# Feed-forward and transposes as pairs of 64-row tiles, read-out levels as 64x64 tiles, early inverses by doubling, with a new instruction order

## The chip, the core and the metric

The kernel runs on one core of a Trainium2 chip. A core has five engines with instruction streams of their own: TensorE (PE) for matrix products, whose weight loads the profile lists apart as PEld; VectorE (DVE); ScalarE (ACT); GpSimd (POOL); and SyncE (SP), which here only issues DMAs. They synchronise through semaphores. PE writes its results to PSUM, and DVE and ACT bring them from there to SBUF. The metric is device time in microseconds (us), the median of several runs.

## The reference

The first half is a recurrence over 768 tokens, for 4 batches of 8 heads (32 sequences), with a 40x40 state for each:

```python
for t in range(S):
    y[:, :, t] = np.einsum('bhd,bhde->bhe', rt, state)
    Sa = np.einsum('bhde,bhe->bhd', state, at)
    state_decay = state * wt[:, :, None, :] - np.einsum('bhd,bhe->bhde', Sa, bt)
    state = state_decay + np.einsum('bhd,bhe->bhde', vt, kt)
```

The second half takes `y` as 3072 rows of 320 numbers and is a gated feed-forward with 1536 hidden units:

```python
rms = np.sqrt(np.mean(x * x, axis=-1, keepdims=True) + 1e-06)
xn = x / rms * rms_g
g = xn @ w_gate
silu = g * (1.0 / (1.0 + np.exp(-g)))
val = xn @ w_val
return (silu * val @ w_out).astype(np.float32)
```

The four weight inputs are 64-bit floats and everything else is 32-bit. The kernel turns the weights into 32-bit floats itself.

## The kernel before

**Chunks.** The tokens are cut into 24 chunks of C = 32. For each chunk, all 32 sequences are handled together: a tile's 128 partitions hold two halves (`half`, 64 partitions) of two sets of 32 tokens, or 40-wide vectors at partitions 0 to 39 and 64 to 103 (`part`).

`front(c)` prepares a chunk. It loads w, a, k, b, v by DMA, transposes them on PE (`turned`, eight transposes of 128 rows in one piece called a turn), and makes Gram products (`gramk`, 32 products of 40 rows by 64 columns in each of four pieces), from which DVE picks, with `where`, the 32x32 triangular matrix `LT` of each sequence, level by level (`LEVELS` = 1, 2, 4, 8, 16). Between levels DVE and ACT scale and copy the decayed keys `K` and `A`.

`inverse(c)` inverts the triangular matrices by forward substitution on DVE, 31 steps of two operations each, with DMAs through DRAM that put one sequence on each row and back. For the first four chunks (`EARLY`) `early_inverse(c)` does two halves of 16 so, 15 steps, and joins them on PE with two pieces of small products.

`main(c)` applies a chunk. On PE it makes the pieces "state", "lower" (twice), "update", three turns (r, every second chunk; `VU`; the state `ST`), "score", five read-out "level" pieces and "y0". A level piece multiplies 128 rows: `As` holds the masked scores of both halves with zeros between (`msi` is the mask), so 16 products of 128 rows and 40 columns do a level. `down` adds the levels into `y` on DVE. Then `y` is transposed (`turn4`), normalised on ACT, and transposed again (`turn3`) into `xg`.

**Feed-forward.** `feed(g)` takes the 256 rows of two chunks. There are 12 slices of 128 hidden units, two at a time. For each slice the weights (480 KB) come by DMA from `sW` in DRAM. The 320 inputs are two full blocks of 128 rows and one of 64: the pieces "h64" (gate and value side by side as two 64-row tiles) and "h" (four products of 128 rows), with 256 columns moving. ACT makes the Silu, DVE multiplies (`hT`), and "out" adds two products of 320 moving columns into the PSUM tile `po`. A product of 32-bit floats shows in the trace as two matmul records, a transpose as one.

**Narrowing.** `narrow` makes the 32-bit weights, in 24 pieces of 480 columns: DMA in, three ACT operations, three DVE operations, and DMA out to `sW`. `narrow_slice(f)` is called from the first `feed`.

**What sets the order.** Nothing is issued where it is written. `Plan.add` records each piece with what it reads and writes, and `Plan.issue` plays all pieces in the order of a table of numbers, `ORDER`; a "-" there is a warm-up product on PE (line 1015). `PAIRS` says which of three double PSUM banks (`ps`) a piece uses. Engines take their instructions in that order, each waiting on semaphores. Since helper functions issue everything, the profile names few lines: 444 for DVE's tensor operations, 467 and 470 for ACT's copies and scalings, 486 for products, 489 for transposes, 483 for DMAs.

Of the kernel before, what the change touches and what calls it, by code (L numbers as in the profile page):

```python
# [21 lines left out]
WB = 5  # L22
LEAD = 2
# [10 lines left out]
85 83 84 76 58 78 86 74 73 59 60 75 5 89 61 88 77 4 43 6 201 7 87 334 90 44 8 214 213 53 62 9 - - - - - - - - 93 18 10  # L34
567 335 557 11 12 13 79 14 15 94 566 80 210 16 95 558 108 17 200 - - - 97 96 19 20 100 21 2 22 101 23 98 25 568 202 24
26 107 112 57 - - - - - 102 106 111 124 27 209 122 392 103 109 52 119 113 104 54 578 569 577 155 199 125 110 105 204
120 - - - - - - 114 203 118 117 121 559 211 598 589 562 46 131 129 132 45 560 212 597 563 588 561 123 115 136 586 384
133 134 - - - - - 126 130 116 47 564 3 145 216 394 383 135 336 128 137 48 144 143 141 91 587 219 142 51 570 127 1005
565 146 138 337 55 573 579 281 393 220 582 608 571 390 234 239 607 572 583 580 380 574 251 222 38 221 609 575 581 42 -
- - - - - - - 223 82 226 339 64 379 227 338 39 81 139 224 263 149 576 238 153 56 249 247 590 206 584 228 382 237 591  # L40
593 272 40 233 232 381 154 0 593 32 139 390 204 228 591 388 234 249 247 - - 324 235 35 31 27 244 229 146 147 259 281
245 258 149 34 325 594 36 33 270 155 243 62 605 584 598 230 - 239 40 214 599 601 242 628 64 49 91 627 602 30 626 1135
600 28 48 257 603 29 241 68 150 255 65 0 1347 194 0 194 84 173 0 - - - 182 540 200 0 184 1 186 542 540 0 506 0 457 469
849 199 455 242 111 97 110 112 96 51 61 439 460 458 122 50 243 0 0 255 242 0 709 104 470 242 120 246 259 708 57 247
458 456 0 257 718 256 470 242 0 716 265 487 486 0 268 0 0 265 101 473 0 262 277 0 273 0 236 0 260 0 269 0 242 461 - -
- - - - - 237 0 240 0 278 242 252 0 242 252 0 90 0 0 98 99 246 0 0 230 440 0 230 94 93 457 440 231 - - - - - - - - -
240 441 244 0 44 0 468 440 255 0 450 468 269 469 0 257 214 439 238 213 203 0 257 203 93 449 92 0 0 234 - - - - - - - -
245 437 0 250 262 0 464 246 247 436 260 245 446 258 259 469 244 - - 255 471 465 468 470 466 0 269 215 255 478 466 93
94 264 95 96 266 97 0 97 470 1 2 98 99 0 0 96 467 97 469 98 468 251 265 99 470 100 471 101 441 102 103 258 104 105 260
106 - - - - - - - - - - - 0 106 107 471 108 0 108 502 503 472 0 108 109 110 111 0 0 0 0 0 - - 13 0 16 562 572 146 571  # L50
561 147 14 142 143 374 15 13 355 - - - 25 386 358 0 358 386 388 16 25 387 389 390 70 79 17 391 28 191 147 355 356 80
148 149 359 0 68 28 2 29 149 0 149 34 150 29 151 187 24 25 31 152 33 153 188 391 393 32 154 35 390 392 358 0 0 152 40
187 153 27 154 155 156 33 157 158 159 160 161 34 162 36 163 164 37 165 41 391 38 42 392 39 394 561 166 395 393 552 0
42 559 549 548 395 209 0 549 560 42 165 210 43 44 211 427 428 395 - - - 565 166 45 167 557 168 0 565 566 168 739 0 522
# [189 lines left out]
class Plan:  # L244
# [17 lines left out]
    def foot(self, ap):  # L262
# [9 lines left out]
        if key not in self.masks:  # L272
# [4 lines left out]
            self.masks[key] = m  # L277
        return p, p + dims[0][1], self.masks[key]

    def add(self, engine, kind, issue, outs, ins):  # L280
        me = len(self.pieces)
        k = self.count.get(self.stage, 0)
        self.count[self.stage] = k + 1
# [85 lines left out]
def kernel(  # L369
# [440 lines left out]
    def main(c):  # L810
# [120 lines left out]
        if c % CG == 0:  # L931
            xg[c // CG] = xg_.next()
# [115 lines left out]
```

## Time and profile before

| | |
|---|---|
| median of 3 runs | 1065.89 us (1064.65 to 1071.17) |
| span of the profiled execution | 1060.6 us |
| first feed-forward's result leaves PSUM | 238.7 us |
| tenth, eleventh, twelfth | 953.6, 1014.0, 1055.2 us |
| TensorE clock granted, mean | 0.979 |

A row of a group has the line, engine, operation, the tile written and the tiles read, the shape (rows by columns of the weights, then partitions by elements of what moves) and the count; behind the bar stand the busy time in us, the mean duration of one in ns, and the idle time of the engine just before, with what ended it. A row of the timeline has the start in us, the length, and how many equal records were merged; in brackets is the idle time before and what ended it. "issue" there means that the engine waited for nothing that the profile shows. In a row by windows the engines stand in the order PE, PEld, DVE, ACT, POOL, then the granted clock, the busy share of the DMA engines and GB/s.

### The profile page before, as it was taken

The page shows a single profiled execution, that of the slowest core. Times are in us where ns is not written, and L with a number is a line of the kernel's source. Part 1 is how long each engine was busy: PE and PEld are TensorE (multiplying, and loading weights), DVE is VectorE, ACT ScalarE, POOL GpSimd, SP SyncE. Part 2 cuts the span into 40 slices and gives each one's busy share as a digit, 9 for nine tenths or more (in the row PEclk, how much of TensorE's full clock was granted, in tenths as well). Part 3 has the DMA queues.
Part 4 walks back from the last instruction along what each step waited for, and adds up shares of the span by engine and source line. Part 5 has one row for each costly group of instructions (what it writes and reads, how often), then busy time and mean ns, then how long its engine had stood idle before and what let it go on. Part 6 is the DMA issues. An engine that isn't in the chain of part 4 may idle for free.

```text
span 1060.6 us, 53494 instructions
## 1 busy us (share of the span) xinstructions
PE 1009.5 (95%) x23406; PEld 829.3 (78%) x23406; DVE 842.3 (79%) x2861; ACT 468.1 (44%) x1043; POOL 309.5 (29%) x554
## 2 busy tenths in 40 slices
PE   7868999999999999999999999999999999999997
PEld 6767777777888778787778778787777888787875
DVE  8978878776868988898898798989889899787411
ACT  6856666643543534434443444434344443431211
POOL 8824413120532241241233241340331331110000
PEclk9777998999999999999999999999999999999999
DMA  9965458766565483655565555574555555443252
GB/s 168 216 155 133 77 127 207 211 123 178 127 140 126 106 173 96 150 134 125 123 155 129 135 132 114 122 160 119 137 126 126 138 137 138 100 132 102 80 162 68
DMA packets 172457, 143.35 MB, mean 135 GB/s; under 512 B 125504, under 2 KB 143872, under 8 KB 172224
## 3 DMA queue, kind: packets, MB, share of 16 engines
q1 hardware_dynamic: 153856, 116.96, 42.9%
q0 software_dynamic: 16192, 22.64, 12.1%
q8 instruction: 184, 3.01, 1.2%
q10 hardware_dynamic: 2176, 0.33, 0.3%
q14 instruction: 49, 0.40, 0.1%
HBM read 123.86 MB, written 15.99 MB: 132 GB/s over the span
## 4 chain that ended last, share of the span: by engine, by line
PE 72%; DVE 8%; DMA 4%; ACT 3%; issue 3%; POOL 2%; SPq 1%; DVEq 0%; ACTq 0%; POOLq 0%
PE ps L486 50%; PE po L486 13%; PE ps L489 8%; DMA wf<-sW 2%; DVE LT L444 1%; DVE y L444 1%; DVE tmp L444 1%; POOL kbn L483 1%; DVE Yi L444 1%; DVE K L444 1%; SPq L483 1%; DMA sY<-Yi 1%; ACT VU L467 1%; PE po L1015 0%; DVE Ab L444 0%
## 5 line engine op out<-in xcount | busy, mean ns | idle before, releaser
L486 PE MATMUL ps<-xg,wf 128*128 128x256 f32 (+1 forms) x1728 | 353.5, 390 | 4.0 <-DVE xg L444 2.0
L486 PEld LDWEIGHTS ps<-xg,wf 128*128 128x128 f32 (+1 forms) x1728 | 261.4, 188 | 57.2 <-issue 15.0
L486 PE MATMUL po<-wf,hT 128*128 128x320 f32 x576 | 183.1, 449 | 0.1
L464 ACT ACTIVATE sg<-ps 128x256 f32<-128x256 f32 x144 | 53.6, 382 | 228.2 <-PE ps L486 224.9
L444 DVE TENSOR_TENSOR tmp<-Yi,M 128x60 f32<-128x60 f32 (+24 forms) x620 | 130.7, 211 | 19.1 <-DMA M<-sB 5.9
L444 DVE TENSOR_TENSOR Yi<-Yi,tmp 128x60 f32<-128x60 f32 (+24 forms) x620 | 129.7, 209 | 12.7
L483 POOL DMA_DIRECT2D VU<-in_v_dram x92 | 53.2, 584 | 274.1 <-PE ps L486 141.8
L486 PEld LDWEIGHTS po<-wf,hT 128*128 128x128 f32 x576 | 102.5, 191 | 35.7 <-issue 4.1
L444 DVE TENSOR_TENSOR hT<-ps,sg 128x256 f32<-128x256 f32 x144 | 59.7, 420 | 67.2 <-ACT sg L464 66.4
L444 DVE TENSOR_TENSOR K<-K,T 128x512 f32<-128x512 f32 (+1 forms) x192 | 93.4, 496 | 8.3 <-PE ps L486 5.8
L486 PEld LDWEIGHTS ps<-Ab,K 40*64 40x64 f32 x4608 | 77.2, 138 | 28.1 <-issue 10.5
L467 ACT COPY K<-K 128x256 f32<-128x256 f32 (+1 forms) x168 | 71.7, 443 | 58.4 <-PE ps L486 39.2
L486 PE MATMUL ps<-Ab,K 40*64 40x56 f32 x4608 | 87.2, 224 | 9.7 <-issue 3.8
L444 DVE TENSOR_TENSOR As<-ps,msi 128x256 f32<-128x256 f32 (+1 forms) x186 | 78.9, 476 | 14.4 <-PE ps L486 13.8
L467 ACT COPY KN<-ps 128x640 f32<-128x640 f32 x96 | 66.1, 690 | 53.5 <-PE ps L489 23.3
L483 POOL DMA_DIRECT2D kbn<-in_b_dram x92 | 53.3, 583 | 96.7 <-PE ps L486 94.3
L486 PEld LDWEIGHTS ps<-As,KN 128*40 128x40 f32 x3072 | 66.5, 124 | 15.7 <-issue 10.4
L483 POOL DMA_DIRECT2D kbn<-in_k_dram x92 | 53.6, 585 | 82.7 <-PE ps L486 82.6
L486 PE MATMUL ps<-As,KN 128*40 128x32 f32 x3072 | 73.2, 205 | 3.1 <-issue 2.5
L483 POOL DMA_DIRECT2D wn<-in_w_dram x92 | 51.6, 567 | 62.7 <-DVE tmp L444 24.1
L444 DVE TENSOR_TENSOR y<-y,ps 128x256 f32<-128x256 f32 x119 | 50.0, 420 | 16.2 <-PE ps L486 13.7
L444 DVE COPY_PREDICATED LT<-near,ps 128x384 f32<-128x384 uint32 (+2 forms) x72 | 52.2, 725 | 2.6 <-PE ps L486 2.0
(133 smaller groups left out, 1546.0 us busy)
## 6 DMA issues: line engine op xcount, KB each, us to landing
wf<-sW SPq DMA_DIRECT2D x144, 480.0 KB, 3.9
M<-sB SPq DMA_DIRECT2D x80, 128.0 KB, 4.1
rn<-in_r_dram SPq DMA_DIRECT2D x24, 160.0 KB, 5.4
sW<-ex SPq DMA_DIRECT2D x16, 240.0 KB, 3.4
out_dram<-o SPq DMA_DIRECT2D x48, 80.0 KB, 4.2
kbn<-in_k_dram POOLq DMA_DIRECT2D x92, 40.0 KB, 3.9
kbn<-in_b_dram POOLq DMA_DIRECT2D x92, 40.0 KB, 4.1
wan<-in_a_dram POOLq DMA_DIRECT2D x46, 80.0 KB, 4.9
```

Source lines behind the costliest of these rows:

```text
L444: plan.add("DVE", kind, lambda at: fn(at(o), *m(at)), [o], aps(*args))
L464: plan.add("ACT", "act", lambda at: nc.scalar.activation(at(o), at(a), f, **kw), [o] + aps(acc), [a])
L467: plan.add("ACT", "copy", lambda at: nc.scalar.copy(at(o), at(a)), [o], [a])
L483: plan.add(by, "dma", lambda at: queue.dma_start(out=o, in_=i), [o], [i])
L486: return o, lhsT, rhs, lambda at: nc.tensor.matmul(at(o), lhsT, rhs, start=start, stop=stop, skip_group_check=True)
L489: return o, i, ident, lambda at: nc.tensor.transpose(at(o), i, ident)
```

## The change

**Feed-forward.** The 320 inputs become five blocks of 64 (`KC`), and gate and value stand in the two halves of the partitions, so that each product has 64 rows and goes in a pair with the one of the other half. The value half meets its blocks in another order, so `xg` holds each block in both halves; three DMAs per two chunks copy them across. "out" becomes "oa" and "ob": each half of `hT`'s rows is multiplied apart, once for its own bank of `po` and once crossed.

```diff
-            pe("h64", [mm(h[e][:, q], wk[e][4][half(q)], x[half(q), 2, :], e == 0, False) for e in range(2) for q in range(2)],
-               [hh])
...
-                pe("h", [mm(h[e][:, q], wk[e][2 * q + kt], x[:, kt, :], False, kt == 1)
-                                           for q in range(2) for kt in range(2)])
-                act(sgs[:, e], h[e][:, 0], AF.Silu)
-                tt(hTs[:, e], h[e][:, 1], sgs[:, e], MUL)
-                pe("out", [mm(po[:, q, 0:DM], hTs[:, e, q * P:(q + 1) * P], wfs[e][:, 2 * P:2 * P + DM], f + e == 0, f + e == FT - 1)
-                                            for q in range(CG)])
+        def proj(k, cross, first, last):
+            wfs, hT = done[k]
+            return pe("o" + "ab"[cross], [mm(po[:, r ^ cross, 0:DM], hT[half(r), e * GT + (r ^ cross) * P:e * GT + (r ^ cross) * P + P],
+                                             wfs[e][half(r), KC * P:], first and e == 0, last and e == 1)
+                                          for e in range(2) for r in range(2)])
...
+                pe("h", [mm(hh[:, r, e * GT:(e + 1) * GT], wfs[e][half(r), s * P:(s + 1) * P], x[half(r), s], e == 0 and s == 0, e == 1 and s == KC - 1)
+                         for s in range(KC) for r in range(2)], [] if e else [hh], [Y[k - 2]] if e and k > 0 else [])
+            act(sg, hh[:, 0], AF.Silu)
+            tt(hT, hh[:, 1], sg, MUL)
+            Y[k - 1] = proj(k, k % 2, k == 0, False)
+            if k:
+                Y[k - 1] = proj(k - 1, k % 2, False, False)
+        copy(still, po[0:1, :, 0:1])
+        proj(KF - 1, 1 - (KF - 1) % 2, False, True)
```

```diff
+        if c % CG == CG - 1:
+            x = xg[c // CG]
+            dma(x[half(0), 1:4:2], x[half(1), 0:3:2])
+            dma(x[half(1), 1:4:2], x[half(0), 0:3:2])
+            dma(x[half(1), 4], x[half(0), 4])
```

**Transposes.** Each one is cut into its two halves of rows, 64 (or 40) each; `turn4` and `turn3` likewise.

```diff
-        pe("turn", [flip(ps[0:outs, at(n), 0:ins], t[0:ins, n, 0:outs], ident[0:ins, 0:ins]) for n in range(N)])
+        pe("turn", [flip(ps[0:outs, u, at(n), 0:w], t[by(u), n, 0:outs], ident[by(u), by(u)]) for n in range(N) for u in range(2)])
```

**Read-out levels and Gram products.** A level takes 32 products of 64 rows, 40 columns and 16 moving columns in place of 16 of 128 rows and 32 moving columns; `As` is half as large, its mask `ms` has no zeros, and `down` adds the three middle levels in two halves. The Gram products from level 4 on load 60, 56 and 48 columns in place of 64.

```diff
-            pe("level", [mm(ps[part(o), slot(n)], z["KN"][LEVELS[j]][:, kn_at(LEVELS[j], n, o)],
-                              As[:, j, o * N + slot(n)].rearrange("p i t -> p (i t)")) for n in range(N) for o in range(2)])
+            pe("level", [mm(ps[part(o), i, slot(n)], z["KN"][LEVELS[j]][half(i), kn_at(LEVELS[j], n, o)],
+                            As[half(i), j, o * N + slot(n)]) for n, i, o in each])
...
-            pe("gramk", [mm(gr[half(i), o, n, 0:16 + D], K[part(o), 2 * n + i].rearrange("p x s -> p (x s)"),
+            pe("gramk", [mm(gr[i * 64:i * 64 + 64 - l, o, n, 0:16 + D], K[part(o), 2 * n + i].rearrange("p x s -> p (x s)")[:, 0:64 - l],
```

**Early inverses.** The first four chunks' inverses are made by doubling, five rounds of two PE pieces and two DVE operations, with no DMA.

```diff
+        for j in range(len(LEVELS)):
+            ps = plan.room()
+            pe("inv", [mm(ps[other(i, n), o, n % 4 * C:(n % 4 + 1) * C], LT[other(i, n), o * N + slot(n)], YZ[other(i, n), o, 1, n % 4] if j else one(other(i, n)))
+                       for n, i, o in by_q])
+            tt(W, ps[:, :, 0:4 * C].rearrange("p o (m t) -> p o m t", m=4), msk[:, j:j + 1, None].to_broadcast((P, 2, 4, C)), MUL)
...
+            pe("inv", [mm(ps[other(i, n), o, at(w, n)], *[x[other(i, n), o, n % 4] if x is W or j else one(other(i, n)) for x in ((W, YZ[:, :, 0]) if w == 0 else (YZ[:, :, 0], W))])
+                       for w in range(ws) for n, i, o in by_q])
...
+            tt(yz, yz if j else eye32[:, None, None].to_broadcast((P, 2, 8, C)), ps[:, :, 0:ws * 4 * C].rearrange("p o (m t) -> p o m t", t=C), SUB)
```

**Narrowing and buffers.** A slice is narrowed in three pieces of 384, 256 and 320 columns in place of two of 480, `WB` (weight buffers) goes from 5 to 6, and Silu and product take both slices at once.

**Order.** `ORDER` and `PAIRS` are new throughout:

```diff
 ORDER = """
-85 83 84 76 58 78 86 74 73 59 60 75 5 89 61 88 77 4 43 6 201 7 87 334 90 44 8 214 213 53 62 9 - - - - - - - - 93 18 10
...
+492 8 9 10 11 - - - 12 - 13 14 15 16 17 18 19 20 21 649 401 - - - 22 - 48 - 36 487 499 - 500 46 498 - 58 - 59
...
```

On PE, in the middle of the program, around the turn of `VU` of one chunk, the order before reads (a row is a line, an operation, the tiles, the shape written, and how often it stands there in a row):

```order
692 L486 MATMUL po<-wf_167,hT_174 128x320 x2
693 L489 MATMUL ps_76<-ident,VU_114 104x128 x8
694 L486 MATMUL ps_75<-Ab_145,K_141 64x56 x32
695 L486 MATMUL ps_77<-VU_114,KN_0_133 40x40 x32
696 L486 MATMUL po<-wf_168,hT_175 128x320 x2
697 L486 MATMUL po<-wf_169,hT_175 128x320 x2
698 L489 MATMUL ps_76<-ident,ST_117 104x104 x8
699 L489 MATMUL ps_77<-ident,K_141 128x104 x8
700 L486 MATMUL ps_75<-Ab_144,K_142 64x56 x32
701 L486 MATMUL ps_77<-rE_154,vut_103 64x32 x32
702 L486 MATMUL ps_76<-xg_166,wf_170 128x256 x2
703 L486 MATMUL ps_76<-xg_166,wf_171 128x256 x2
```

The order now, at the turn of `VU` of such a chunk:

```order
758 L519 MATMUL po<-wf_174,hT_177 128x320 x2
759 L522 MATMUL ps_76<-ident,VU_115 104x64 x16
760 L519 MATMUL ps_77<-VU_115,KN_0_134 40x40 x32
761 L519 MATMUL ps_75<-Ab_146,K_142 56x56 x32
762 L519 MATMUL ps_76<-rE_155,vut_103 64x32 x32
763 L519 MATMUL ps_77<-Ab_145,K_143 48x56 x32
764 L519 MATMUL ps_75<-ST_118,aP_148 32x40 x32
765 L519 MATMUL ps_75<-VU_116,LT_120 32x40 x32
766 L519 MATMUL ps_76<-As_159,KN_0_131 40x16 x32
767 L519 MATMUL ps_76<-rE_155,Sd_137 40x32
```

Before, feed-forward pieces (`po`, `xg`) stand between the pieces of the chunk at rows 696, 697, 702 and 703; now none stands from row 759 on until row 786 (row 767 is the first of the 32 products of "y0", rows 784 and 785 are a level and a turn).

Near the start, on PE, an early inverse before is two pieces among warm-ups (`po<-ident`):

```order
37 L1015 MATMUL po<-ident 128x128 x11
38 L486 MATMUL ps_77<-M_148,LT_118 16x16 x32
39 L486 MATMUL ps_76<-M_148 32x16 x32
40 L1015 MATMUL po<-ident 128x128 x2
41 L486 MATMUL ps_75<-Xs_156,M_148 32x40 x32
```

Now it is a row of pieces of 32 and 64 products, with Gram pieces of other chunks between:

```order
23 L519 MATMUL ps_75<-ident,M_149 32x32 x32
24 L519 MATMUL ps_75<-M_149,ident 32x32 x32
25 L519 MATMUL ps_77<-VU_115,LT_119 32x40 x32
26 L519 MATMUL ps_75<-M_149,LT_119 32x32 x32
27 L519 MATMUL ps_77<-Ab_146,K_142 60x56 x32
28 L519 MATMUL ps_76<-M_149 32x32 x64
```

The number of small products ahead of a given place of the program rises by these.

On SP the copies of the swapped halves stand among the weight loads of the next feed-forward:

```order
150 L516 DMA M_150<-sB_182 32x1024 x3
151 L516 DMA xg_168<-xg_168 64x256
152 L516 DMA xg_168<-xg_168 64x2x256 x2
153 L516 DMA wf_172<-sW_66 128x960
154 L516 DMA wf_171<-sW_65 128x960
```

Before, no such rows exist; the loads of `M` and `wf` follow each other there.

More of the change, by code (lines that the diff above doesn't have):

```diff
@@ L494, in issue @@
                 s[3](at)
-        plan.add("PE", kind, issue, [s[0] for s in steps] + more, [x for s in steps for x in s[1:3]])
+        return plan.add("PE", kind, issue, [s[0] for s in steps] + more, [x for s in steps for x in s[1:3]], after)
     ident = const.tile([P, P], FP32, name="ident")
@@ L939, in feed @@
+    Y = {}
     def feed(g):
```

359 lines of the change are left out of this document (166 added, 193 removed), and 336 rows, old and new, of the table ORDER.

## The prediction

> **What bounds the kernel now.** The page comes first: its span, the share of each engine, the instruction queue, and the chain that ended last by engine.
>
> ```profile
> span 1060.6 us, 53494 instructions
> PE 1009.5 (95%) x23406; PEld 829.3 (78%) x23406; DVE 842.3 (79%) x2861; ACT 468.1 (44%) x1043; POOL 309.5 (29%) x554
> q8 instruction: 184, 3.01, 1.2%
> PE 72%; DVE 8%; DMA 4%; ACT 3%; issue 3%; POOL 2%; SPq 1%; DVEq 0%; ACTq 0%; POOLq 0%
> ```
>
> TensorE (PE) is busy for 95% of the span and 72% of the chain. A view by windows then cuts the span into a start, a middle and an end (for each engine its busy time and, as x, its records).
>
> ```profile
> 0.00:240.00 240.00, 210.30 (x5275) 180.01 (x5276) 194.83 (x616) 151.65 (x321) 101.34 (x198) 0.91 0.69 158
> 240.00:960.00 720.00, 704.10 (x16848) 575.11 (x16847) 612.86 (x2149) 298.75 (x682) 207.09 (x354) 1.00 0.55 132
> 960.00:1061.00 101.00, 95.13 (x1286) 74.20 (x1284) 34.58 (x96) 17.68 (x42) 1.10 (x2) 1.00 0.35 104
> ```
>
> In the middle PE is busy 704 of 720 us and VectorE (DVE) 613; a chunk has 256+64+160+64+64+64+128+51 = 851 PE records and a feed-forward 192, so two chunks with their feed-forward take 720x1,894/16,848 = 81 us. So PE sets the time, and what a PE record costs decides the change. That is read from the timeline, not from the mean of a group, since records overlap: I divide the distance between starts by the count. First the pure feed-forward at the end (weight loads, one per product).
>
> ```profile
> 1030.57 0.73 PEld L486 LDWEIGHTS ps<-xg,wf 64*128 64x128 f32 x8 [0.44 <-issue]
> 1031.64 0.83 PEld L486 LDWEIGHTS po<-wf,hT 128*128 128x128 f32 x4 [0.33 <-issue]
> 1032.55 5.21 PEld L486 LDWEIGHTS ps<-xg,wf 128*128 128x128 f32 x24
> 1037.79 2.02 PEld L486 LDWEIGHTS po<-wf,hT 128*128 128x128 f32 x8
> 1040.25 1.13 PE L486 MATMUL ps<-xg,wf 64*128 64x256 f32 x8
> ```
>
> Whole-array products go at (1037.79-1032.55)/24 = 0.218 us. The eight 64-row products take 1031.64-1030.57 = 1.07 us: four pairs at 0.218 are 0.87, so the two row halves do run together, and 0.20 is left for the change of tile shape ("issue" in the row).
>
> Then the small products, in the middle and near the start.
>
> ```profile
> 446.09 0.81 PE L486 MATMUL ps<-Ab,K 40*64 40x56 f32 x40
> 447.43 0.57 PE L486 MATMUL ps<-Ab,K 40*64 40x56 f32 x24 [0.53 <-issue]
> 447.82 0.81 PE L486 MATMUL ps<-VU,KN 64*40 64x40 f32 x64
> 448.56 1.99 PE L486 MATMUL ps<-xg,wf 128*128 128x256 f32 x8
> 450.39 1.04 PE L489 MATMUL ps<-ident,VU 128*104 128x128 f32 x8
> 451.36 0.57 PE L486 MATMUL ps<-Ab,K 40*64 40x56 f32 x24
> 452.54 0.81 PE L486 MATMUL ps<-Ab,K 40*64 40x56 f32 x40 [0.61 <-issue]
> 453.17 1.09 PE L486 MATMUL ps<-rE,vut 40*64 40x32 f32 x64
> ```
>
> ```profile
> 111.80 0.64 PE L486 MATMUL ps<-As,KN 128*40 128x32 f32 x22
> 112.85 0.99 PE L486 MATMUL ps<-As,KN 128*40 128x32 f32 x41 [0.41 <-issue]
> 113.65 0.20 PE L486 MATMUL ps<-As,kbn 128*40 128x32 f32 x1
> 113.67 0.20 PE L486 MATMUL ps<-As,KN 128*40 128x32 f32 x1
> 113.69 0.80 PE L486 MATMUL ps<-As,kbn 128*40 128x32 f32 x31
> 114.42 0.55 PE L489 MATMUL ps<-ident,x 128*128 128x128 f32 x3
> 114.89 1.18 PE L486 MATMUL ps<-As,KN 128*40 128x32 f32 x51
> 116.30 0.45 PE L486 MATMUL ps<-As,KN 128*40 128x32 f32 x13 [0.22 <-issue]
> ```
>
> Here is the row that decides. PE stops inside a run of equal products that wait for nothing ("issue"). From one stop to the next, 112.85 to 116.30, stand 41+1+1+31+3+51 = 128 records; from 447.43 to 452.54 stand 24+64+8+8+24 = 128 again. The instruction queue moved 184 transfers for 23,406 products, one per 127 products with their weight loads. So PE's instructions arrive in blocks of about 127 products, and where a block is used up before the next is there, PE stands. In the lower stretch nothing but supply ended the stops, and a block took 116.30-112.85 = 3.45 us, or 0.027 us a product. By themselves small products go faster: 64 in 448.56-447.82 = 0.74 us, 40 in 453.17-452.54 = 0.63, thus 0.012 to 0.016, and 0.014 is my mean. This kernel escapes since one product in ten belongs to the feed-forward at 0.2 us or more, and in its order these pieces stand among the small ones.
>
> **The change part by part.** First PE, as if instructions cost nothing.
>
> *Turns* (transposes). A chunk has 5x8+4+4+3 = 51 of them, 8 in 451.36-450.39 = 0.97 us with a change of shape, so 0.11 each, 24x51x0.11 = 135 us. They become 102 half as long, in pairs. A pair costs 0.055 if only the moving length counts, 0.11 if the load of 104 to 128 columns does. The run of 40 above loads, in each row half, 128 columns (two tiles of 64) per four products, in 4x0.016 = 0.063. I take 0.06: 24x51x(0.11-0.06) = 61 us less (bounds 0 and 67).
>
> *Changes of tile shape.* The order of all PE rows has 531 before and 443 now: 88x0.20 = 18 us less. The new order still alternates between 64x128 and 64x64, so no more goes.
>
> *Trimmed Gram products.* 64 load columns become 60, 56 and 48; at 0.063 us per 128 columns that is 16x56x0.063/128 = 0.44 us a chunk, 10 us.
>
> *Read-out levels.* 160 records a chunk become 320. Today 31 start in 114.42-113.69 = 0.73, thus 0.023 each, 3.7 us; the nearest row of the new shape is the 64x40 one, 0.74/64 = 0.0116, again 3.7 us. I take 0.
> The Trainium skill, page "TensorEngine Tiling (Array Packing)", section "Theoretical Speedup", promises up to 2x from a second small dimension; by it the levels would give 24x3.7/2 = 44 us, and the time would be 1078. The 64x40 row speaks against it: at 0.0116 a product four tiles take as long as two do now.
>
> *Feed-forward products.* Ten 64-row pairs replace eight whole products and two pairs; by the 1.07 us row a pair costs what a whole one does, so 0. Three copies per two chunks (the swapped halves) go on SP's queue; the next feed-forward waits for them, and in the order pieces of the previous feed-forward and of chunks still stand ahead of it. Cost 0; about 4 us each time if that cover were gone, as for a copy of this size on that queue:
>
> ```profile
> M<-sB SPq DMA_DIRECT2D x80, 128.0 KB, 4.1
> ```
>
> The copy into `still` puts one wait on ACT and then PE at each feed-forward's end; behind it are ACT's next copies and PE's last eight products of that feed-forward, and chunk pieces stand around both. Cost 0.
>
> *DVE.* The rows:
>
> ```profile
> L444 DVE TENSOR_TENSOR As<-ps,msi 128x256 f32<-128x256 f32 x144 | 54.1, 416 | 4.8 <-PE ps L486 4.2 <-ACT As L470 0.4
> L444 DVE TENSOR_TENSOR As<-ps,msi 128x512 f32<-128x512 f32 x42 | 28.4, 683 | 9.6 <-PE ps L486 9.6
> L444 DVE TENSOR_TENSOR hT<-ps,sg 128x256 f32<-128x256 f32 x144 | 59.7, 420 | 67.2 <-ACT sg L464 66.4
> L444 DVE TENSOR_TENSOR Ab<-Ab,T 128x128 f32<-128x128 f32 x96 | 27.0, 289 | 1.2 <-PE ps L486 0.3 <-ACT Ab L467 0.2
> ```
>
> As falls from 54.1+28.4 to 24x4x0.416+18x0.42 = 47.5 (-35); hT to 72x0.683 = 49.2 (-10.5); the level sums split at three levels, 72x(2x0.289-0.42) = +11. Narrowing the same elements in 36 instead of 24 pieces adds 12x3 steps, at most 12x3x0.289 = 10 us, in the start. DVE goes to about 808 to 818 us. Per two chunks of the middle it is 81x612.86/720 = 69 now, 66 then, below PE's 81-89/12 = 74. It doesn't take over.
>
> *Early inverses.* Their 30 short DVE steps and the DMA round trips become PE products, (5x32+4x64+32)x4 = 1,792 or 3,584 records instead of 512, all before the middle; their price is in the start, below.
>
> Sum without a limit on instructions: 61+18+10 = 89 us less. The start (5,275 records, about five chunks) keeps its waits, so 19/24 of it counts, 71.
>
> Now the supply. A chunk goes from 851 records to 256+64+320+64+64+64+128+102 = 1,062, a feed-forward from 192 to 336. All: 24x1,062+12x336+3,584+252 warm-ups, less what chunk 0 lacks, about 33,200, which is 261 blocks. Spread evenly they would fit: 261x3.45 = 900 us. The order doesn't spread them. In the old order only one stretch without a feed-forward piece is over 264 records, the one before the first feed-forward. In the new one 35 more are over 254, with 13,388 records together, and the one shown with the change, from row 759, is 608 long. A stretch starts with about one block in hand; beyond it a product costs 0.027 instead of 0.014: (13,388-35x127)x0.013 = 116 us more. Who waits for that: the ACT and DVE steps that empty PSUM, which have room (44% and 79% busy).
>
> The start, with the first feed-forward product and the warm-ups that fill its waits:
>
> ```profile
> 130.27 1.14 PE L486 MATMUL ps<-xg,wf 64*128 64x256 f32 x8
> L1015 PE MATMUL po<-ident 128*128 128x128 f32 x302 | 48.0, 311 | 3.7 <-DVE po L517 3.3 <-issue 0.4
> ```
>
> The old order has 2,828 records ahead of that product, at 130 us. The new one has 5,800: 5,800/127x3.45 = 158 us if supply ends last throughout, so +28; 0 if the waits that hold PE today stay the longer. I take +22.
>
> Sum: 1060.6-71+116+22 = 1128; the median of the runs shown (1065.89) lies 5.3 above the profiled span, so 1133. Some stops will fall where PE waits today (16 us of the middle), 11 of them say: 1122.
>
> **The rivals.**
>
> *Supply hides.* The stops inside runs are rare today (all "issue" before weight loads, changes of shape included):
>
> ```profile
> PEld ps L486 <- issue: 62.4, 157, 2.0
> ```
>
> If the blocks come in time whenever PE isn't starved for other reasons, the time is 1060.6-89+5 = 977 to 1060.6-71+5 = 995, with DVE at 66 of 74 us close behind, so 970 to 1000. It decides from the point at which 127 products take as long as their supply: above 0.027 a product nothing stops. Against it: stops exactly 128 records apart, and 35 stretches that run at half of that.
> The Trainium skill, "Runtime: NRT & Kernel Launch", section "Instruction fetch mechanics", says that instructions come in blocks of 256 into a buffer of two, and that the crossing is mostly hidden. The trace agrees with the blocks (184 transfers for 46,812 loads and products are 254 each) and, by the rows above, not with the hiding in runs of small products. Chance 0.17.
>
> *Supply and today's waits overlap more than I count.* Half of the 116 and nothing at the start: 1060.6-71+58 = 1048, 1053 as a median, 1025 to 1075. Chance 0.15, half of it within 1%.
>
> *Nothing overlaps.* Every small product is paid at 0.027: 29,200 records outside the feed-forward x0.027 = 788, and of feed-forward 144 slices x (10x0.218+4x0.27) = 470, with 0.27 from the eight of row 1037.79 less a change of shape: 1,258 us. It decides where feed-forward pieces are held by PSUM or by the swapped copies. Against it: a block is always fetched during a feed-forward piece. Chance 0.05; or the turns' pairs not halving, 1122+61 = 1183, chance 0.05.
>
> **How the numbers follow.** Forecast 0.58 (1080 to 1170: supply cost from 75 to 150, turns and levels by their bounds). Slower by over 1%, which is about what a measurement tells from no change: 0.58+0.10 = 0.68. Within 1%: 0.08. Faster: 0.17+0.07 = 0.24. The likeliest alone spans 1080 to 1170; for 8 in 10 the range reaches down into the second rival and up to the turns' bound, 1010 to 1185, and leaves out the hidden supply and the case where nothing overlaps, 0.2 at most.
>
> **What would show it.** About 261 instruction transfers; PE "issue" stops near 128 records apart inside runs of levels and Gram products, longest in the stretch after a feed-forward, near 150 us together against 62; turns of 16 in about 0.5 us; no shape stops inside a feed-forward. DVE busy near 808 us and no longer close to PE's bound. It is wrong if runs of several hundred small products pass at 0.014 us each, if the middle falls below 75 us per two chunks, or if DVE or a DMA ends the chain's waits.

## The result, and the profile after

The changed kernel takes 1385.51 us (median of 4, 1381.15 to 1395.61) against 1068.53 for the one before on the same chip: ratio 1.2975, 95% interval 1.2905 to 1.3046. The profiled execution spans 1379.6 us, 319.0 more than before. Forecast were 1122 us: slower was right, and so were the number and the spacing of the instruction blocks, but the size was too small by more than 250 us, beyond even the rival in which nothing overlaps (1258).

The page of the kernel after, the lines that answer to those of before:

```profile
span 1379.6 us, 72886 instructions
PE 1119.2 (81%) x33212; PEld 941.1 (68%) x33212; DVE 813.4 (59%) x2745; ACT 451.3 (33%) x1025; POOL 302.9 (22%) x532
q8 instruction: 260, 4.26, 1.3%
PE 64%; issue 17%; DVE 12%; DMA 3%; ACT 2%; POOL 1%; SPq 1%; DVEq 0%; ACTq 0%; POOLq 0%
```

The 260 instruction transfers and DVE's 813 us are as forecast. But "issue" is 17% of the chain where it was 3%, and PE is busy for 110 us more than before although it should have had less to do. To see why, I cut both spans at the first output product of the first feed-forward (139 us before, 214 after). These are the windows of the kernel before, then of the kernel after (us, then busy time and records of PE, PEld, DVE, ACT, POOL, then the granted clock, DMA share and GB/s):

```profile
0.00:139.00 139.00, 114.16 (x3108) 101.97 (x3108) 116.63 (x355) 91.68 (x192) 76.28 (x155) 0.86 0.68 144
139.00:1061.00 922.00, 895.37 (x20305) 727.35 (x20298) 725.63 (x2508) 376.40 (x852) 233.24 (x399) 1.00 0.55 134
```

```profile
0.00:214.00 214.00, 157.04 (x5972) 142.17 (x5974) 113.75 (x291) 95.87 (x212) 64.70 (x126) 0.66 0.44 98
214.00:1380.00 1166.00, 962.13 (x27244) 798.92 (x27240) 699.61 (x2455) 355.47 (x813) 238.15 (x406) 0.85 0.45 108
```

Three things changed. The start is 75 us longer. In the rest PE stands (is not busy) for 1166-962 = 204 us instead of 922-895 = 27, which is 177 more. And the granted clock, 1.00 before, is 0.85. The clock record of the trace has no values but 1.0 and 0.5, so a mean of 0.819 over the span (0.979 before)

```profile
core 0: 1379.6 us, clock 0.819
```

means 2x(1-0.819)x1379.6 = 499 us at half clock, against 45 before ("half clock" below is this product). This is what a stop and half clock look like in the timeline of PE after (rows left out at the dots):

```profile
564.33 4.48 PE L519 MATMUL ps<-xg,wf 64*128 64x256 f32 x40
...
582.85 2.06 PE L519 MATMUL ps<-As,KN 64*40 64x16 f32 x109 [1.24 <-issue]
584.83 0.92 PE L522 MATMUL ps<-ident,ST 40*104 40x40 f32 x16
585.54 1.20 PE L519 MATMUL ps<-xg,wf 64*128 64x256 f32 x2
588.84 5.89 PE L519 MATMUL ps<-xg,wf 64*128 64x256 f32 x38 [2.10 <-issue]
```

Between the two stops stand 109+16+2 = 127 records, one block, but they took 588.84-582.85 = 5.99 us, not 3.45. And behind the stop 38 feed-forward records take 5.89 us, 0.155 each, where 40 take 4.48 or 0.112 at full clock (row 564.33). In the waits of the whole kernel after, these are the rows for PE's instructions (us in total, times, longest). Before, they were 62.4 and 16.9 us; the forecast for the first was near 150:

```profile
PEld ps L519 <- issue: 243.1, 187, 5.6
PE ps L519 <- issue: 200.9, 112, 5.5
```

From 40 to 200 us the start is held by the supply of instruction blocks alone: of the 49 us that PE stands there, 48 end with "issue". 4,990 records in 160 us are 4.07 us per 127, at a clock of 0.58.

```profile
40.00:200.00 160.00, 111.43 (x4990) 100.59 (x4994) 72.37 (x189) 65.74 (x152) 30.99 (x54) 0.58 0.33 83
```

### The profile page after: what moved, and what is told of

It reads as the page before. It is cut to its first block, busy times and chain, and to the rows that moved or that the text cites. A ratio compares the mean times of both kernels' runs of the same rounds, so it can differ in the third digit from the quotient of the medians.

```text
span 1379.6 us, 72886 instructions
## 1 busy us (share of the span) xinstructions
PE 1119.2 (81%) x33212; PEld 941.1 (68%) x33212; DVE 813.4 (59%) x2745; ACT 451.3 (33%) x1025; POOL 302.9 (22%) x532
## 4 chain that ended last, share of the span: by engine, by line
PE 64%; issue 17%; DVE 12%; DMA 3%; ACT 2%; POOL 1%; SPq 1%; DVEq 0%; ACTq 0%; POOLq 0%
PE ps L519 44%; PE po L519 11%; PE ps L522 6%; PE po L1042 3%; DVE Yi L477 3%; DVE tmp L477 2%; DVE LT L477 2%; DMA wf<-sW 1%; DVE hT L477 1%; DMA M<-sB 1%; DVE K L477 1%; ACT sg L497 1%; SPq L516 1%; DVE VU L477 0%; DVE Ab L477 0%
## 5 line engine op out<-in xcount | busy, mean ns | idle before, releaser
L519 PE MATMUL ps<-xg,wf 64*128 64x256 f32 x2880 | 368.8, 406 | 11.9 <-issue 4.8
L519 PEld LDWEIGHTS ps<-xg,wf 64*128 64x128 f32 x2880 | 303.5, 203 | 53.9 <-issue 7.7
L519 PE MATMUL po<-wf,hT 64*128 64x320 f32 x1152 | 215.3, 505 | 17.9 <-DVE hT L477 13.7
L519 PEld LDWEIGHTS po<-wf,hT 64*128 64x128 f32 x1152 | 120.1, 214 | 63.7 <-issue 18.2
L519 PE MATMUL ps<-As,KN 64*40 64x16 f32 x6144 | 96.8, 202 | 54.0 <-issue 53.5
L519 PEld LDWEIGHTS ps<-As,KN 64*40 64x40 f32 x6144 | 89.0, 142 | 64.8 <-issue 60.4
L519 PE MATMUL ps<-Ab,K 40*60 40x56 f32 (+2 forms) x4608 | 97.6, 241 | 30.4 <-issue 27.6
L519 PEld LDWEIGHTS ps<-Ab,K 40*60 40x60 f32 (+2 forms) x4608 | 84.9, 150 | 46.6 <-issue 36.1
L477 DVE TENSOR_TENSOR hT<-ps,sg 128x512 f32<-128x512 f32 x72 | 49.6, 688 | 94.7 <-ACT sg L497 93.9
L477 DVE TENSOR_TENSOR y<-y,ps 128x128 f32<-128x128 f32 (+1 forms) x191 | 55.8, 317 | 78.5 <-PE ps L519 63.0
```

Of the source, the lines that this page charges most:

```text
L477: plan.add("DVE", kind, lambda at: fn(at(o), *m(at)), [o], aps(*args))
L519: return o, lhsT, rhs, lambda at: nc.tensor.matmul(at(o), lhsT, rhs, start=start, stop=stop, skip_group_check=True)
```

## The experiments

All carry the time of the kernel before on the same chip beside them (1058 to 1066 us); ratios are to that. The expectations name the theories: supply (blocks come too slowly, and the clock is halved behind the stops), order, tiles, clock. Half clock is worked out from each run's mean clock and span, as above.

**One part at a time in the old order.** `b_gram`: `K...[:, 0:64 - l]` in the Gram products, and no more. `b_turn`: that, and

```diff
-        pe("turn", [flip(ps[0:outs, at(n), 0:ins], t[0:ins, n, 0:outs], ident[0:ins, 0:ins]) for n in range(N)])
+        pe("turn", [flip(ps[0:outs, u, at(n), 0:w], t[by(u), n, 0:outs], ident[by(u), by(u)]) for n in range(N) for u in range(2)])
```

> The kernel before with the trimmed Gram products alone, in its own order and with its own count of records. By the weight columns that are left out 10 us less, ratio 0.985 to 0.995; if a small product's time is set by something else than its load columns, 0.995 to 1.005.

> The kernel before, in its own order, with two parts of the change alone: the transposes as pairs of 64-row tiles (1,224 PE records more, 24,630 in all) and the trimmed Gram products. Supply theory (PE's instructions come in blocks of about 127 products; stops appear only where runs of small products use blocks up faster than 3.45 us, and the clock is halved behind them): this order spreads its records, so few stops are added; 1,000 to 1,050 us, 194 instruction transfers, half clock for under 70 us (45 before, 498 after). Tile theory (the two row halves don't run together, so a pair of turns costs two whole ones): 24x51x0.11 = 135 us more, 1,150 to 1,210. Order theory (the new order loses the time by its waits, whatever the count): 1,000 to 1,060.

`b_gram` gave 1056.11 us, 0.9948 (0.9915 to 0.998): some 5 us, half of the 10 that the load columns gave and on the border of the two ranges. It is the only version here that is faster than both kernels, by half a per cent. `b_turn` gave 1100.96, 1.0407 (1.0337 to 1.0478), outside all three ranges that I had given to it. The turns do halve (in the kernel after, 16 stand between 500.24 and 500.79 us, 0.55 us against 0.97 for 8). In this order they bring 652 changes of shape for 531, and 1,224 records, and half clock rises from 45 to 141 us. How the 42 us divide among these isn't shown.

`b_lev`, the levels alone, and `b_all`, levels, turns, Gram and

```diff
-                pe("h", [mm(h[e][:, q], wk[e][2 * q + kt], x[:, kt, :], False, kt == 1)
-                                           for q in range(2) for kt in range(2)])
+                pe("h", [mm(h[e][:, r], wk[e][2 * r + kt][half(r)], x[half(r), kt, :], False, kt == 1 and cross == 1)
+                                           for cross in range(2) for kt in range(2) for r in range(2)])
```

> The kernel before, in its own order, with the read-out levels alone as 64x64 tiles without the zeros (3,840 PE records more, 27,246 in all; the level sums and the masked scores as in the change). Supply theory: runs of 64 level products become 96 and more, two a chunk; 1,100 to 1,200 us, 214 instruction transfers, stops inside the runs of levels, half clock for 100 us or more. Order theory: no new wait, less work on VectorE; 1,045 to 1,075. Tile theory: four tiles take turns, 0.023 us each: 24x320x0.023 = 177 against 88, about 1,150, but without stops and at full clock.

> The kernel before, in its own order, with all parts of the change that alter the count in the middle: turns as pairs, trimmed Gram products, levels as 64x64 tiles, and each whole feed-forward product as two 64-row ones on the two row halves (their sums come out other than in the reference). 30,500 PE records; not in it are the doubling inverses, the narrowing and the new order. Turns with Gram cost 42 us alone and levels 141. Parts theory (the count of small records makes the loss, feed-forward pairs too): 1,290 to 1,350, so that order and start make under 100 of the 320. Order theory (feed-forward pairs cost nothing, as a pair takes as long as a whole product): 1,220 to 1,260, so that the new order with its longer start makes 130 to 160.

`b_lev`: 1199.83, 1.135 (1.1257 to 1.1442), half clock 222 us. This is the supply theory's case, at the upper end of its range, and DVE's 24 us less (818) buys nothing. `b_all`: 1236.84, 1.1588 (1.1458 to 1.1719). Its windows:

```profile
0.00:153.00 153.00, 123.72 (x3604) 110.42 (x3607) 113.76 (x359) 91.55 (x202) 75.91 (x155) 0.71 0.57 131
153.00:1229.00 1076.00, 939.38 (x26601) 765.23 (x26592) 703.16 (x2574) 375.02 (x890) 233.58 (x399) 0.89 0.46 115
```

So with almost the count of the new kernel in the middle (26,601 records of 27,244) the old order loses 14 us in the start and 154 behind it. The rest, some 150 us, lies in what `b_all` leaves out: the order, the first inverses, the narrowing and the swapped copies. No run takes these apart.

**Fewer records in the new order.** `a_lev`: levels as 16 whole-height products; `a_all`: also turns and feed-forward products whole.

```diff
-            pe("level", [mm(ps[part(o), i, slot(n)], z["KN"][LEVELS[j]][half(i), kn_at(LEVELS[j], n, o)],
-                            As[half(i), j, o * N + slot(n)]) for n, i, o in each])
+            pe("level", [mm(ps[part(o), n % 2, slot(n)], z["KN"][LEVELS[j]][:, kn_at(LEVELS[j], n, o)],
+                            As[:, j, o * N + slot(n)]) for n in range(N) for o in range(2)])
```

> The kernel after, in its own order, with the read-out levels as whole-height products of the same 16 columns, half as many (3,840 PE records fewer, 29,372); half of each level's places aren't written, all else stays. Supply theory: 1,170 to 1,280 us, and half clock falls from 498 to 250 to 400 us. Order theory: 1,360 to 1,390. Tile theory: 88 us less, about 1,300, the clock as in the kernel after.

> The kernel after, in its own order, with levels, turns and feed-forward as whole-height products (26,130 PE records instead of 33,212; the sums and places come out other than in the reference). Supply theory: most of the loss goes, 1,020 to 1,120 us, half clock under 200 us. Order theory: 1,300 or more. Tile theory: as the supply theory in time, but the same share of half clock as the kernel after.

`a_lev`: 1291.67, 1.2207 (1.2092 to 1.2321), near the tile theory's 1,300, with half clock at 424 us. But four tiles don't take turns, since `micro` (below) runs 128 such products in 1.41 us, 0.011 each. `a_all`: 1265.46, 1.1959 (1.1855 to 1.2063), between the supply theory and the order theory. Its windows show that there is a cause beside the count, the order or something else that `a_all` keeps of the change:

```profile
0.00:192.00 192.00, 152.83 (x5463) 139.57 (x5464) 112.69 (x290) 95.52 (x212) 64.72 (x126) 0.73 0.46 108
192.00:1262.00 1070.00, 945.73 (x20678) 786.72 (x20678) 700.56 (x2456) 356.86 (x814) 237.95 (x406) 0.91 0.46 117
```

20,678 records, the count of before (20,305), take 1070 us instead of 922: 1070-946 = 124 us of standing for 27, and a clock of 0.91 for 1.00.

**The same records, dealt otherwise.** `a_spread`, `a_split2` and `a_split` change where the feed-forward pieces stand, and give out the PSUM banks as they come free. The core of `a_split2` (`a_split` has 127 and 64 for 192 and 96):

```diff
+            if small > 6000 and run >= 192 and near is not None and at[near] - small > 96:
+                while near not in done and ready(feed[0]):
+                    go(feed.pop(0))
```

> The kernel after with the same instructions and the same 33,212 PE records, and one thing changed: the pieces of each feed-forward are dealt evenly among the chunk pieces instead of where the order table has them (everything else keeps its order; PSUM pairs are given out as they come free). Runs of over 254 small records without a feed-forward product fall from 35 to 6, the records beyond the first 127 of each run from 10,052 to 5,117 (before: 1,803); changes of tile shape rise from 443 to 550. Supply theory (stops where a run uses blocks up faster than they come, and the halved clock behind the stops): 1,170 to 1,250 us, half clock under 280 us of 498. Count theory (the number of records matters, wherever they stand): 1,370 to 1,400. Order theory in its other form (the searched order hides DVE, ACT and DMA waits, which this one opens): 1,390 or more.

> The kernel after with the same records, and the next feed-forward piece drawn forward into a run when 192 small records have gone by and over 96 more stand before it (all else keeps its order). Runs over 254 records go from 35 to 21, the records beyond the first 127 of each run from 10,052 to 7,700, shape changes from 443 to 488. By the four kernels so far that keep a searched order (before, levels alone, levels whole, after) a record beyond the first 127 costs 0.039 us: 92 us less, 1,280 to 1,330. If such an order costs by other waits: 1,380 or more.

> The same, drawn forward after 127 small records where over 64 more follow: 14 runs over 254 (the longest 672), 5,603 records beyond the first 127, 535 changes of shape. Supply theory: 170 us less and 18 for the shapes, 1,210 to 1,290. If pieces drawn forward wait for ACT and DVE as in the evenly dealt order: above 1,390, with waits of feed-forward products on DVE's hT of 40 us and more.

`a_spread` gives each piece a place of its own, `at = a + (b - a) * (q // 2 * 2) / pes`, between the first pieces of two feed-forwards. All three were slower than the kernel after: 1684.01, 1426.01 and 1429.19 us (1.5847, 1.3455 and 1.3485). In the evenly dealt one the stops for supply did shrink (240 to 1000 us: 21.2 us of "PE ps <- issue" for 107.1), but PE now waits for DVE's `hT`, which the output products need:

```profile
PE po L566 <- DVE hT L523: 42.9, 19, 9.6
PE ps L566 <- issue: 21.2, 17, 3.6
PE ps L566 <- DVE hT L523: 14.0, 10, 1.5
```

The clock of `a_spread` fell further:

```profile
core 0: 1682.5 us, clock 0.775
```

That is 757 us at half clock for 499, so fewer stops for supply did not bring the clock back while PE stopped for other waits. My price of 0.039 us for each record beyond the first 127 of a run, which fitted four kernels, fell here: runs made shorter in this way don't give the time back. That the clumps of the new order (small products in long runs without a feed-forward piece) are what costs is thus argued from `a_all`, not shown by undoing them.

**The block by itself.** `micro` and `micro2` compute no part of the reference. PE alone runs equal products, for instance:

```python
    for cols in (16, 64, 128):
        small(508, cols)
        big(64)
```

> No part of the reference is computed: PE alone runs stretches of 508 equal small products (1,016 records, 8 blocks) of 64x40 weights moving 16, 64 and 128 columns, each followed by 64 whole products of 256 columns; then 40 times 32 small and 2 whole; then 889 small ones with big loads on two queues beside them; then 508 of 128x40. Supply theory: the 16 and 64 column stretches take 8x3.45 = 28 us or a little more with stops 127 to 128 records apart, the 128 column one 28 us almost without stops, and the first whole products behind the 16 column stretch run at half clock for 3 us or more; the mixed stretch (a whole pair per 64 small records) runs without stops. With loads beside it a block takes over 4 us if instructions queue behind data, 3.45 if not. If stops come from the kernel's waits and not from supply: no stops here, and 1,016 records in 14 us.

> No part of the reference is computed: runs of 762 small products (1,524 records, 12 blocks) of 64x40 moving 24, 32, 40 and 48 columns with 64 whole products behind each; then 1,143 small ones of 17 and 18 columns beside loads of 960 KB one at a time on one queue; then 12 times 127 small of 16 columns (254 records) with 4 whole products of 250 behind them, and the same with 26 columns. Activity theory: a width between 16 and 64 from which the clock stays full, all runs at 3.45 us a block. If blocks queue behind data by its amount: 3.45 without loads, 6.2 at 360 GB/s, thus about 4.2 to 4.8 at 100 to 180 GB/s. In the stretches of 254 small and 8 whole records a block's fetch is hidden by 8x0.22 us at most: (254x0.011+1.7) = 4.5 us of work against 262/127x3.45 = 7.1 of supply, so 7.1 a round; if one block in hand hides the stop, 4.5 to 5.5.

The timeline of `micro` at 16 columns, at 64, at 128, at 18 with the loads beside, and at 32 with 128 rows (rows left out at the dots):

```profile
39.18 2.33 PE L32 MATMUL small<-X,W 64*40 64x16 f32 x223
43.30 1.41 PE L32 MATMUL small<-X,W 64*40 64x16 f32 x128 [1.79 <-issue]
46.76 2.33 PE L32 MATMUL small<-X,W 64*40 64x16 f32 x128 [2.04 <-issue]
50.21 2.33 PE L32 MATMUL small<-X,W 64*40 64x16 f32 x128 [1.13 <-issue]
...
94.64 3.44 PE L32 MATMUL small<-X,W 64*40 64x64 f32 x231
...
102.60 2.00 PE L32 MATMUL small<-X,W 64*40 64x64 f32 x128 [1.46 <-issue]
106.05 2.00 PE L32 MATMUL small<-X,W 64*40 64x64 f32 x128 [1.46 <-issue]
...
148.64 27.94 PE L32 MATMUL small<-X,W 64*40 64x128 f32 x1016
...
325.01 2.33 PE L32 MATMUL small<-X,W 64*40 64x18 f32 x128 [3.86 <-issue]
331.20 2.34 PE L32 MATMUL small<-X,W 64*40 64x18 f32 x128 [3.86 <-issue]
...
409.77 2.64 PE L32 MATMUL small<-X,W 128*40 128x32 f32 x128 [0.83 <-issue]
```

Where PE stops, 128 records stand from stop to stop, with nothing in the kernel to wait for. A block takes 50.21-46.76 = 3.45 us; products of 128 columns, 27.87/1016 = 0.0274 us each, just need no stop. Beside the loads it takes 331.20-325.01 = 6.19. The last row has the shape that a level had before: it fills 2.64 us of a block and leaves a stop of 0.83, where the new shape (16 columns) leaves 2.04. Only the first run of a stretch is longer, 215 to 271 records in the two kernels (223 and 231 above): behind 64 whole products, about two blocks were in hand. Here are windows of `micro` over these stretches and over 40 rounds of 32 small products with 2 whole ones (the fourth row), then of `micro2` at 24, 40 and 48 columns and beside one load at a time:

```profile
46.76:64.30 17.54, 11.64 (x640) 11.11 (x640) 0.00 (x0) 0.00 (x0) 0.00 (x0) 0.50 0.02 5
99.14:120.42 21.28, 11.97 (x769) 11.04 (x770) 0.00 (x0) 0.00 (x0) 0.00 (x0) 1.00 0.02 5
148.64:176.51 27.87, 27.87 (x1017) 27.68 (x1017) 0.00 (x0) 0.00 (x0) 0.00 (x0) 1.00 0.01 4
204.34:278.43 74.09, 71.69 (x2718) 55.44 (x2717) 0.00 (x0) 0.00 (x0) 0.00 (x0) 1.00 0.02 4
325.01:343.62 18.61, 7.00 (x384) 6.66 (x384) 0.00 (x0) 0.00 (x0) 0.00 (x0) 0.50 1.10 363
```

```profile
42.33:77.42 35.09, 23.37 (x1282) 22.16 (x1282) 0.00 (x0) 0.00 (x0) 0.00 (x0) 0.50 0.02 5
182.72:214.35 31.63, 20.37 (x1152) 19.08 (x1152) 0.00 (x0) 0.00 (x0) 0.00 (x0) 0.55 0.02 5
254.30:282.76 28.46, 12.54 (x1024) 11.51 (x1025) 0.00 (x0) 0.00 (x0) 0.00 (x0) 1.00 0.02 5
319.12:344.66 25.54, 11.67 (x640) 11.11 (x640) 0.00 (x0) 0.00 (x0) 0.00 (x0) 0.50 0.62 192
```

A block costs 3.45 us beside 5 GB/s of data, 25.54/5 = 5.1 beside 192 and 6.2 beside 363. Stops of some 2 us halve the clock at 16, 24 and 40 columns (rows 43.30 and 46.76: 1.79 and 2.04 us before the halving, 1.1 once the products take longer), and stops of 1.9 to 2.2 us at 48 columns and up to 2.0 at 64 don't. The mixed rounds kept PE busy for 71.69 of 74.09 us at full clock.

254 small records with 8 whole ones behind them took (496.28-410.65)/11 = 7.8 us a round at 16 columns (starts of the first and the twelfth). At 26 columns and full clock a round took 551.89-544.88 = 7.0:

```profile
544.88 2.28 PE L32 MATMUL small<-X,W 64*40 64x26 f32 x187
551.89 2.21 PE L32 MATMUL small<-X,W 64*40 64x26 f32 x181
```

That is what supply alone asks, 262/127x3.45 = 7.1. So blocks are fetched during a short feed-forward piece too, but at this mix the round still pays for every block in full.

`a_wf` takes the question of the loads into the kernel: it leaves out the weight loads from the third feed-forward on (8 columns of each remain).

```diff
-                dma(wf, sW[2 * k + e])
+                dma(wf[:, 0:WF if g < 2 else 8], sW[2 * k + e][:, 0:WF if g < 2 else 8])
```

> The kernel after without the loads of feed-forward weights from the third feed-forward on (8 columns of 960 are loaded; the products use what the buffers hold). If instruction blocks come late because they queue behind these loads: the longest stops after 240 us fall from 5.5 to under 3.5 us, and the time to 1,270 to 1,340. If a block costs what it costs alone: stops as before, 1,360 to 1,390.

`a_wf`: 1322.43 us, 1.2447 (1.2349 to 1.2545), some 60 us less. Behind the start PE stands for 162 us instead of 204:

```profile
208.00:1325.00 1117.00, 954.57 (x27244) 793.39 (x27244) 699.21 (x2456) 355.52 (x814) 237.80 (x406) 0.86 0.28 60
```

The time is the one of the theory that blocks queue behind data, but the longest stop stayed (6.3 us for 5.5), so these loads aren't what makes the longest.

**The clock.** `a_warm` puts useless products in:

```diff
+                run = 0 if p.key[0] == "feed" else run + p.n
+                if run > 127:
+                    for _ in range(6):
+                        self.warm()
+                    run -= 127
```

> The kernel after with useless work put in: after every 127 small records without a feed-forward product six warm-up products of 192 columns (0.16 us and two records each; 1,032 in all, 2,064 records). Clock theory (the halved clock is a cost of its own, beside the stops, and comes from PE being busy for too small a share of a few us): half clock falls from 498 to under 200 us, and the time stays or falls, 1,300 to 1,390, although the records cost 2,064x0.027 = 56 us more. If only the stops cost time and the clock is nothing: 1,440 to 1,550.

`a_warm`: 1489.58 us, 1.4021 (1.3913 to 1.4128), in the range of "the clock is nothing". But I had priced a warm-up product at less than half of what it takes (0.16 us for 2x309.3/1568 = 0.39, since each product has two records). These are its window behind the start and its group of warm-ups there (busy time, mean ns, idle before):

```profile
242.00:1485.00 1243.00, 1143.58 (x28780) 970.19 (x28776) 698.40 (x2451) 353.52 (x810) 237.79 (x406) 0.97 0.40 102
```

```profile
L1050 PE MATMUL po<-ident 128*128 128x192 f32 x1568 | 309.3, 348 | 18.5 <-issue 18.0 <-ACT still L506 0.3
```

The clock is back at 0.97, and without the warm-ups PE is busy 1143.6-309.3 = 834 us; the kernel after needs 962.1-9.0 = 953 for the same products (9.0 us of its own warm-ups taken off in the same way). So half clock makes PE busy for some 119 us more there. The stops fall too, from 204 to 1243-1144 = 99 us, and `a_warm` is slow because it pays 309 us to win these.

Not all of the 119 need be lost time. The feed-forward products alone (those with the tile `wf`) have this in the kernel after, then in `a_warm`:

```profile
214.00:1380.00 1166.00, 568.88 (x3992) 417.53 (x3988) 15.16 (x36) 6.40 (x11) 0.85 0.45 108
242.00:1485.00 1243.00, 512.70 (x3992) 379.88 (x3988) 13.50 (x32) 5.89 (x10) 0.97 0.40 102
```

They account for 56 us. The other 63 lie in the small products and in how records that overlap the warm-ups are counted. In `micro` a block of small products takes 3.45 us at either clock (46.76-43.30, where the clock falls, and 50.21-46.76): there a slower product only fills a part of the stop. How much of the 63 falls in such blocks isn't shown.

`a_wide` puts useless columns in:

```diff
+                    nc.tensor.matmul(at(out), kn[half(i), kn_at(LEVELS[j], n, o)], A(n, i, o)[:, None].to_broadcast((64, w, 16)),
+                                     start=True, stop=True, skip_group_check=True)
```

> The kernel after with useless columns: each level product writes its 16 columns again into the blocks of its PSUM slot that are still free (32 to 64 columns instead of 16), and each score product moves 64 instead of 32. Same records, same order, same values. Activity theory (the clock halves when the array is busy for too little of a few us; the stretch of 64 columns kept full clock with the very stops that halved it at 16): half clock falls from 498 to 300 to 440 us and the time by 20 to 60, 1,325 to 1,365. If the stops themselves halve the clock: half clock as before, 1,380 to 1,400; if longer products simply cost: 1,400 or more.

`a_wide`: 1371.98, 1.2963 (1.2884 to 1.3042), no difference from the kernel after. Half clock fell only from 499 to 464 us, which misses the activity theory's range. Wider levels and scores are less than a third of the small records (9,216 of 29,180); whether they are too few, or whether the columns don't count in this way, the run doesn't tell.

## Why the prediction was wrong

*Where the 319 us come from.* The start makes 214-139 = +75; standing behind it +177; PE's longer busy time at half clock +119; and PE's work, taken from `a_warm` at a clock of 0.97, 834 us for 895.4-11.0 = 884, makes -50. The sum is 321; the 2 us over are warm-ups.

*PE bound, turns, shapes, Gram, levels, feed-forward (-89, of which 71 counted).* The direction was right, and the size is -50 by `a_warm`. Turns of 16 in 0.55 us and feed-forward records at 0.112 without a stop of shape inside are as forecast; the Gram columns gave 5 us, not 10.

*DVE, swapped copies, the `still` wait.* DVE took 813 us for 808 to 818, and the copies' waits are 2.7 us ("PE ps <- DMA xg<-xg"). That is right in the main: DVE's share of the chain rose from 8% to 12%, but behind the start PE's output products waited only 13.7 us for `hT`.

*Supply in the runs (+116, less 11 for overlap).* The mechanism was right, the price was not: 3.45 us a block comes from one stretch and holds only beside almost no data. With the 4.07 us that the start shows, 0.032 a record, the same sum is (13,388-35x127)x(0.032-0.014) = 161, near the 177. The second part of that step, that a stretch begins with about one block in hand, depends on what stands ahead of it: behind 128 whole records `micro` and `micro2` had it (215 to 271 records before the first stop), behind 8 whole records each round still paid for every block.

*The start (+22).* Supply did end last from 40 us on, as in its upper bound; at 4.07 us a block the first 40 us (605 records) and the other 5,367 records make 212 us. Since the 4.07 come from this very stretch, that is no test of the price. I had taken 3.45 and cut it for other waits.

*The clock.* It stood in the view of before (0.91 in the first 240 us), and I read it as a state of the start and gave it no term. It makes some 119 us of busy time, of which the feed-forward's 56 are the surest cost, since its products have few stops that a slower product could fill. This is the graver failure, since it is no size but a missing step. What the runs show in its place: where supply leaves products of 16 to 40 columns 1.4 of every 3.45 us, the clock is granted at half, and the feed-forward behind pays.

The Trainium skill, page "TensorE: Matmul & The Clock Gate", section "What's actually happening", tells of such a gate with the two states that the trace shows, moved by how busy PE was in windows of 3.4 us. The traces agree on the two states. Its rule in the section "HAM oscillation — how this bites in real kernels", no idle gaps above some 3.4 us, would not have warned of the stops that I expected: in `micro` stops of some 2 us halve the clock at 16 columns, and stops of 1.9 us in `micro2` leave it full at 48. Of the stops that came it would have warned only of the longest (5.6 us).

*The rivals.* That supply hides, or overlaps, falls. That nothing overlaps (1258) was nearest and still too low, for the same two reasons. With 4.07 a block and the clock, my own sum would have been 1060.6-50+161+73+119 = 1364 of the 1379.6 measured. That is bookkeeping with prices measured afterwards, and its closeness is in part luck: small products at half clock may be counted in the 161 and again in the 119. With the feed-forward's 56 alone it is 1301.

*What stays open.* How the 148 us that `a_all` loses behind the start (1070 us for 922) divide among the clumps of the order and other things of it, since dealing the pieces otherwise opened new waits; what exactly the clock counts, and how much of the 119 us it costs in time; and what makes the longest stops.

## What to carry to other kernels

Count instructions as a resource: where an engine runs products of 0.01 to 0.02 us, a block of about 127 has a price (3.45 us alone, 4 to 6 beside loads), and splitting a product into more, smaller ones can pay only where enough work stands between them (32 small products to 2 whole ones kept PE busy in `micro`, 127 to 4 did not in `micro2`). Price such a stop twice, once as standing and once as the halved clock of the large products behind it. And take the price of a shared resource from a stretch with the traffic that the changed kernel will have.

## What the runs showed of the hardware

Busy time as the profile counts it isn't what keeps the clock: 16 columns with PE busy 11.64 of 17.54 us (66%) ran at 0.50, 48 columns with 12.54 of 28.46 (44%) at 1.00. Busy time counted at full clock would fit as well as columns: just before the halving a block of 16 columns was busy for 1.41 of 3.45 us (41%). At one block of 64x40 products every 3.45 us, the width from which the clock stays full lies between 40 and 48 columns. Instruction transfers are slowed by data on other queues, from 3.45 to 6.2 us a block at 363 GB/s; in the kernel after, the block of 5.99 us shown above ran beside 191 GB/s (582.85 to 588.84). `micro` and `micro2` ran once each.
